# Low-rank token product in one pass, and channel-product blocks of 512, 512, 512, 512 and 256 tokens

## The chip, the cores and the metric

The kernel runs on one core of one Trainium2 chip. The metric is the device time of one execution in microseconds (us), the median of several runs. The engines are TensorE (PE, with its weight loads PEld), VectorE (DVE), ScalarE (ACT), GpSimd (POOL), and SyncE (SP), which here only issues DMAs.

## What is computed

Three layers run one after the other on 4 batches of 576 tokens and 512 channels: rotary attention with 8 heads, a gated layer with a spatial product over tokens, and a mixer. The change touches only the mixer:

```
xt = x.transpose(0, 2, 1)                 # x: 4 x 576 x 512
h = xt @ U @ V                            # U: 576 x 32, V: 32 x 576
u = x + h.transpose(0, 2, 1)
ch = np.maximum(u @ w_ch1, 0.0) @ w_ch2   # w_ch1: 512 x 2048, w_ch2: 2048 x 512
return u + ch
```

All of it is float32. To come near that on TensorE, an operand is split into a high part (rounded to the type float32r) and a low part (what the rounding left), and a product is made of three matmuls: high by high, high by low, low by high.

## The kernel before

Activations lie with channels on the partitions: `X[b]` holds batch b as 128 partitions x 4 channel groups x 576 tokens. The attention layer comes first, with an order written out by hand for all engines. After it the order of TensorE is the order of the code, and a scheduler, which works at build time with a model of the times, sets the order of the other engines and of the DMA queue.

**The gated layer** goes batch by batch, in steps that are named after their tiles in PSUM: `v` (`v_step`, the normed half, 512 columns a matmul), `u` (`u_step`, the gate), `m` (`s_step`, the spatial product), `w` (`o_step`, the output product). The steps of one batch are interleaved with those of the next.

**The low-rank product** of a batch has three steps. `y_step` transposes X (tile `t`) and splits it into YH and YL. `z_step` multiplies both with `U4` and adds them up in one PSUM tile `z`: U4 holds four groups of 32 columns, so the 128 rows of `z` are four products with 32 columns of U each. In the kernel before the groups are U high, U low, U high, U low. Then Z is made: ACT copies the rows of `z` into the rounded type, and DVE replaces rows 64 to 127 by what the rounding left of them. `h_step` (tile `q`) multiplies Z with V. The host stacks V four times, and `VH4` and `VL4` are its high and its low part over all 128 rows; so one `h_step` takes two matmuls over V high and two over V low, of 288 columns each. DVE then adds `q` to X (L680). There are 4 batches with 4 `h_step`s each.

**The channel products** take the 2304 tokens as five blocks that pay no heed to batches: `WIDE` is 472 four times and 416. The 2048 hidden channels form four groups g of 512. For each group and block, `c1` (tile `r`) makes two halves of 24 matmuls each, ACT and DVE turn them into RH and RL (L738, L739), and `c2` (tile `a`) makes two halves of 24 matmuls each, which DVE adds to X (L754). Each matmul has its own weight load. The code runs `c1` of a block between the two halves of `c2` of the block before. Moving operands are UH/UL (the split X of a block; for block 0 they lie in the old tiles XH/XL) and RH/RL (for group 0 and block 0 in the old VH/VL). Weights lie in setA for groups 0 and 2, and in setB for groups 1 and 3; those of the next group are converted on ACT, DVE and POOL while a group runs. In the last group each piece of X is sent out as it is added.

All PSUM tiles after the attention come from one pool of 4 buffers of two banks each, in turn.

The block sizes stand in the code as

```
WIDE = [472] * 4
WIDE.append(NTOK - sum(WIDE))
```

Of the kernel before, what the change touches and what calls it, by code (L numbers as in the profile page):

```python
# [9 lines left out]
F32R = mybir.dt.float32r  # L10
BF16 = mybir.dt.bfloat16
U32 = mybir.dt.uint32
AF = mybir.ActivationFunctionType
ALU = mybir.AluOpType
# [38 lines left out]
def tile_kernel(ctx: ExitStack, tc: tile.TileContext, qk, vv, tabs, w_in, g_ln, wsgT, b_sg, w_out, u_r, v_r, w1, w2, out):  # L53
    nc = tc.nc

    def f(ap):
        return ap.bitcast(F32)

    def h2(ap):
        return ap.rearrange("p (a b) -> p a b", a=2)  # L60
# [20 lines left out]
    B, NHEAD, _, P, S = qk.shape  # L81
# [23 lines left out]
    keep = ctx.enter_context(tc.tile_pool(name="keep", bufs=1))  # L105
# [3 lines left out]
    XH = keep.tile([P, KT, S], F32R, name="XH")  # L109
    XL = keep.tile([P, KT, S], F32R, name="XL")  # L110
    U4 = keep.tile([P, NC, 4, 32], F32R, name="U4")
    VH4 = keep.tile([P, S], F32R, name="VH4")
    VL4 = keep.tile([P, S], F32R, name="VL4")


    es1 = ExitStack()
# [222 lines left out]
    def converted(t0, src, n, use):  # L339

        raw = p1.tile([P, 512, 2], U32, tag="raw64", name="raw64", bufs=1)[:, :n]
        t = p1.tile([P, 512], F32, tag="t64", name="t64", bufs=1)[:, :n]
        later(t0, lambda: nc.sync.dma_start(raw.rearrange("p n w -> p (n w)"), src))
        for j, fn in enumerate(from_f64(t, raw) + use(t)):
            later(t0 + CONVERT + j, fn)
# [9 lines left out]
    def u_chunk(t0):  # L355
        def use(t):
            t = t.rearrange("p (c r) -> p c r", r=32)
            return sum((
                (lambda j=j: nc.scalar.activation(U4[:, :, 2 * j], t, AF.Copy),
                 lambda j=j: nc.gpsimd.tensor_tensor(U4[:, :, 2 * j + 1], t, f(U4[:, :, 2 * j]), ALU.subtract))  # L360
                for j in range(2)), ())
        converted(t0, u_r, NC * 32, use)

    def v_chunk(t0, a):
        hs = slice(a * HALF, (a + 1) * HALF)
        converted(t0, v_r[:, 2 * a * HALF:2 * (a + 1) * HALF], HALF, lambda t: (
            lambda: nc.scalar.activation(VH4[:, hs], t, AF.Copy),
            lambda: nc.gpsimd.tensor_tensor(VL4[:, hs], t, f(VH4[:, hs]), ALU.subtract),
        ))

    LAG, T0 = 3, -20
# [44 lines left out]
    for a in range(2):  # L416
        v_chunk(WTICK[2 * KT + 1 + a], a)
# [72 lines left out]
    def ps_tile(name):  # L490
        return ps2.tile([P, 2, 512], F32, tag="ps", name=name)
# [48 lines left out]
    def mm3(ps, pairs, halves):  # L540
        n = len(pairs)
        for j, (l, r) in enumerate(pairs):
            for a in range(halves):
                rr = r[:, a * HALF:(a + 1) * HALF] if halves == 2 else r
                o = ps[:, a, :HALF] if halves == 2 else ps
                nc.tensor.matmul(o, l, rr, start=(j == 0), stop=(j == n - 1))  # L546
# [115 lines left out]
    def z_step(b, s):  # L662
        if s == 0:
            ZS[b] = ps_tile(f"z{b}")
        pz = ZS[b]
        u4 = U4[:, s].rearrange("p a r -> p (a r)")
        for j, y in enumerate(YS.pop((b, s))):
            nc.tensor.matmul(pz[:, 0, :], u4, y, start=(s == 0 and j == 0), stop=(s == NC - 1))
        if s == NC - 1:
            Z = p2.tile([P, 2, DM], F32R, tag="YL", name=f"Z{b}", bufs=2)[:, 0]  # L670
            nc.scalar.activation(Z, pz[:, 0, :], AF.Copy)
            nc.vector.tensor_tensor(Z[64:128], pz[64:128, 0, :], f(Z[64:128]), ALU.subtract)
            ZS[b] = Z

    def h_step(b, d):
        Z = ZS[b]
        ps = ps_tile(f"q{b}_{d}")
        ds_ = slice(d * P, (d + 1) * P)
        mm3(ps, [(Z[:, ds_], VH4), (Z[:, ds_], VL4)], 2)
        nc.vector.tensor_tensor(h2(X[b][:, d]), ps[:, :, :HALF], h2(X[b][:, d]), ALU.add)  # L680


# [1 line left out]
    FPG = FG // P  # L684
    NG = DH // FG
    NBLK = 5
    WIDE = [472] * 4
    WIDE.append(NTOK - sum(WIDE))
    flat = lambda t, n: t.rearrange("p a b -> p (a b)")[:, :n].rearrange("p (a b) -> p a b", a=KT)
    UH, UL = [flat(XH, KT * WIDE[0])], [flat(XL, KT * WIDE[0])]  # L690
    W = {}
# [11 lines left out]
    def spans(blk):  # L703

        first = t = sum(WIDE[:blk])
        end = t + WIDE[blk]
        while t < end:
# [13 lines left out]
    def c1(g, blk, i):  # L721

        if i == 0:
            RS[g, blk] = (
                (flat(VH, FPG * WIDE[0]), flat(VL, FPG * WIDE[0])) if (g, blk) == (0, 0) else
                [p3.tile([P, FPG, max(WIDE)], F32R, tag=t, name=t, bufs=2)[:, :, :WIDE[blk]] for t in ("RH", "RL")]
            )
# [52 lines left out]
    for b in range(B - 1):  # L780
# [12 lines left out]
        if n < B - 1:  # L793
            run(y_step, b, 0, 2)
            v_step(n, 4)
            us = iter(range(KT))
            if n % 2:
                u_step(n, next(us))
            run(z_step, b, *range(NC - 1))
            y_step(b, 4)  # L800
            u_step(n, next(us))
            z_step(b, 4)
            u_step(n, next(us))
            run(h_step, b, 0, 1)
            u_step(n, next(us))
            run(h_step, b, 2, 3)
            run(u_step, n, *us)
        else:
            v_step(n, 4)
            w = weights(p2, 0, SETA[2:] + SETA[:2])  # L810
            for k0 in range(KT):
                u_step(n, k0)
                next(w)
    a, b = B - 2, B - 1
    for d in range(KT):
# [3 lines left out]
        if d == 1:  # L819
            u_split(0)  # L820
    run(z_step, a, *range(NC - 1))
    y_step(a, 4)
    c1(0, 0, 0)
    for e in range(KT):
        o_step(b, e)
        next(w)
        if e == 0:
            z_step(a, 4)
    run(h_step, a, *range(KT))
    run(y_step, b, 0, 2)  # L830
    c1(0, 0, 1)
# [87 lines left out]
```

## Time and profile before

| | us |
|---|---|
| median of 3 runs | 974.88 |
| the runs | 973.26, 974.88, 978.32 |
| span of the profiled execution, from its first to its last instruction | 971.3 |
| PE busy | 937.9 (97%) |
| DVE busy | 522.0 (54%) |
| POOL busy | 380.1 (39%) |
| ACT busy | 345.3 (36%) |

The profiled execution shows its own time as the span alone. The median of the runs stands 3.6 us above it; that is taken as what lies around the span. The page's groups give a mean duration of one instruction, and for matmuls that is no pace: one of 472 columns lasts 0.37 us on the page, but the next begins 0.21 us after it, since they overlap. A pace is read from a chain of matmuls: its length over their count. In the trace's names a matmul `q<-VH4,Z` writes tile q from the moving operand VH4 with the weights Z.

### The profile page before, as it was taken

How to read it: one execution, taken by the hardware profiler on the slowest of the kernel's cores; microseconds unless marked ns; L12 is line 12 of the kernel's file. 1: busy time of each engine (PE TensorE's matmuls, PEld its weight loads, DVE VectorE, ACT ScalarE, POOL GpSimd, SP SyncE). 2: the span in 40 equal slices, each digit the busy share in tenths (PEclk: the TensorE clock that was granted, in tenths of full speed). 3: DMA queues.
4: the chain of work that ended last, by engine and by line, in shares of the span. 5: the costliest groups of instructions: out<-in, count | busy, mean ns of one | idle time of the engine just before them, and what ended most of it. 6: DMA issues, size and time to landing. Idle time of an engine off the chain costs nothing.

```text
span 971.3 us, 13254 instructions
## 1 busy us (share of the span) xinstructions
PE 937.9 (97%) x5212; PEld 815.4 (84%) x5212; DVE 522.0 (54%) x721; ACT 345.3 (36%) x549; POOL 380.1 (39%) x325
## 2 busy tenths in 40 slices
PE   6899999999999999999999899999999999999998
PEld 3687777777877888999999798899889988998897
DVE  7777877787774387334328846643552542212222
ACT  4366655665657353323215323221321321010010
POOL 7768777887743495231427533210210120000000
PEclk8999999999999999999999999999999999999999
DMA  6577777777750500000003002220220110000112
GB/s 176 146 183 178 189 195 177 191 195 164 187 116 24 161 26 1 1 1 9 15 23 109 22 22 65 87 65 1 87 87 1 66 44 1 1 1 21 60 40 76
DMA packets 58947, 78.00 MB, mean 80 GB/s; under 512 B 31403, under 2 KB 35270, under 8 KB 58886
## 3 DMA queue, kind: packets, MB, share of 16 engines
q1 hardware_dynamic: 58576, 77.08, 29.3%
q8 instruction: 41, 0.67, 0.3%
q14 instruction: 20, 0.16, 0.1%
q10 hardware_dynamic: 310, 0.08, 0.0%
HBM read 55.02 MB, written 4.79 MB: 62 GB/s over the span
## 4 chain that ended last, share of the span: by engine, by line
PE 75%; DVE 13%; DMA 5%; issue 3%; POOL 2%; ACT 1%; SPq 1%; DVEq 0%; POOLq 0%; ACTq 0%
PE a L546 21%; PE r L546 20%; PE pv L274 10%; PE st L246 6%; PE w L546 5%; PE m L546 3%; PE sm L217 3%; PE u L546 3%; PE v L546 3%; DVE MX L222 2%; DMA Q<-K 2%; DVE X L326 1%; DVE t L75 1%; DVE t L74 1%; DVE t L72 1%
## 5 line engine op out<-in xcount | busy, mean ns | idle before, releaser
L222 DVE TENSOR_REDUCE MX<-sm 128x1 f32<-128x576 f32 (+1 forms) x160 | 118.7, 748 | 60.7 <-PE sm L217 58.0
L274 PE MATMUL pv<-pc,VV 128*65 128x288 f32 x512 | 144.7, 405 | 0.5 <-DVE sums L295 0.5
L246 PE MATMUL st<-Q,K 65*128 65x288 f32 (+3 forms) x640 | 126.9, 320 | 7.6 <-DVE MX L222 5.4
L246 PEld LDWEIGHTS st<-Q,K 65*128 65x128 f32 (+3 forms) x640 | 95.7, 179 | 22.3 <-DVE MX L222 8.3
L738 ACT ACTIVATE RH<-r 128x944 fp32r<-128x944 f32 (+1 forms) x38 | 35.7, 939 | 211.4 <-PE r L546 211.4
L739 DVE SCALAR_TENSOR_TENSOR RL<-r,RH 128x944 fp32r<-128x944 f32 (+1 forms) x38 | 42.5, 1117 | 126.2 <-ACT RH L738 126.2
L249 ACT ACTIVATE pc<-st 128x576 f32<-128x576 f32 x128 | 82.6, 646 | 62.8 <-PE st L246 60.6
L546 PE MATMUL a<-RH,setB 128*128 128x472 f32 (+1 forms) x320 | 95.6, 371 | 0.0
L754 DVE TENSOR_TENSOR X<-a,X 128x416 f32<-128x416 f32 (+4 forms) x65 | 46.4, 745 | 91.0 <-PE a L546 90.9
L274 PEld LDWEIGHTS pv<-pc,VV 128*65 128x65 f32 x512 | 68.6, 137 | 29.5 <-DVE sums L295 0.7
L217 PE MATMUL sm<-K,Q 128*128 128x288 f32 (+1 forms) x320 | 77.0, 325 | 13.1 <-ACT Q L193 5.6
L546 PE MATMUL a<-RH,setA 128*128 128x472 f32 (+1 forms) x288 | 86.0, 370 | 0.0
L546 PE MATMUL r<-UH,setB 128*128 128x472 f32 (+1 forms) x256 | 76.4, 369 | 0.0
L546 PE MATMUL r<-UH,setA 128*128 128x472 f32 (+1 forms) x256 | 76.2, 370 | 0.0
L217 PEld LDWEIGHTS sm<-K,Q 128*128 128x128 f32 (+1 forms) x320 | 50.6, 183 | 23.9 <-ACT Q L193 6.8
L546 PEld LDWEIGHTS a<-RH,setB 128*128 128x128 f32 x320 | 60.2, 188 | 6.9
L510 POOL TENSOR_TENSOR setB<-t,setB 128x512 fp32r<-128x512 f32 x16 | 20.6, 1290 | 103.1 <-ACT setB L699 60.4
L546 PE MATMUL a<-RL,setB 128*128 128x472 f32 (+1 forms) x160 | 59.6, 372 | 0.0
L546 PEld LDWEIGHTS a<-RH,setA 128*128 128x128 f32 x288 | 54.1, 188 | 6.1
L150 POOL TENSOR_TENSOR raw<-raw,tab 128x576 f32<-128x576 f32 x31 | 51.9, 1674 | 4.5 <-DMA raw<-in_qk 4.5
L546 PE MATMUL a<-RL,setA 128*128 128x472 f32 (+1 forms) x144 | 53.4, 371 | 0.0
L149 POOL TENSOR_TENSOR raw<-raw,tab 128x576 f32<-128x576 f32 x30 | 47.6, 1587 | 14.8 <-DMA raw<-in_qk 14.8
(172 smaller groups left out, 1968.0 us busy)
## 6 DMA issues: line engine op xcount, KB each, us to landing
raw<-in_qk SPq DMA_DIRECT2D x31, 576.0 KB
Q<-K SPq DMA_DIRECT2D x87, 144.0 KB
raw<-in_w SPq DMA_DIRECT2D x24, 512.0 KB
VV<-in_vv SPq DMA_DIRECT2D x32, 160.0 KB
rb<-rr SPq DMA_DIRECT2D x15, 288.0 KB
K<-K SPq DMA_DIRECT2D x29, 144.0 KB
raw<-in_w_in SPq DMA_DIRECT2D x8, 512.0 KB
gt<-in_w SPq DMA_DIRECT2D x8, 512.0 KB
```

The costliest lines, as they stand in the source:

```text
L149: lambda: e.tensor_tensor(raw[:, 0], raw[:, 0], tab[:, 0], ALU.mult),
L150: lambda: e.tensor_tensor(raw[:, 1], raw[:, 1], tab[:, 1], ALU.mult),
L217: nc.tensor.matmul(ps[:TS[t], n, :HALF], Q1[:, t * P:t * P + TS[t]], K1[:, n * HALF:(n + 1) * HALF], start=True, stop=True)
L222: nc.vector.tensor_reduce(MXs[h % 2][:TS[t], t:t + 1], ps[:TS[t], :, :HALF], AX.XY, ALU.max)
L246: nc.tensor.matmul(ps[:kk, n, :HALF], l[:, c * P:c * P + kk], r[:, ns], start=st, stop=not st)
L249: nc.scalar.activation(h2(pc[:kk]), ps[:kk, :, :HALF], AF.Exp, scale=0.125)
L274: nc.tensor.matmul(o, l, r, start=(c == 0 and j == 0), stop=(c == NC - 1 and j == len(pr) - 1))
L510: return nc.gpsimd.tensor_tensor(out, a, b, ALU.subtract)
L546: nc.tensor.matmul(o, l, rr, start=(j == 0), stop=(j == n - 1))
L738: nc.scalar.activation(RH[:, s], ps[:, :, :WIDE[blk]], AF.Relu)
L739: nc.vector.scalar_tensor_tensor(RL[:, s], ps[:, :, :WIDE[blk]], 0.0, f(RH[:, s]), ALU.max, ALU.subtract)
L754: nc.vector.tensor_tensor(X[b][:, e2, xs], ps[:, :n, us], X[b][:, e2, xs], ALU.add)
```

## The change

U4's groups become U high, U low, U high, U high. VH4 and VL4 become one tile V4: V high in rows 0 to 95, V low (by a subtraction of 32 rows) in rows 96 to 127. DVE now replaces only rows 64 to 95 of Z by what the rounding left. So the four groups of rows give (U high) by V high, (U low) by V high, the remainder of (U high) by V high, and (U high) by V low, in one pass: one `h_step` has two matmuls where it had four. The remainder of the U low rows is no longer multiplied, nor are the products of the low rows with V low.

The blocks of the channel products are 512 four times and 256.

```diff
     U4 = keep.tile([P, NC, 4, 32], F32R, name="U4")
-    VH4 = keep.tile([P, S], F32R, name="VH4")
-    VL4 = keep.tile([P, S], F32R, name="VL4")
+    V4 = keep.tile([P, S], F32R, name="V4")
...
-            return sum((
-                (lambda j=j: nc.scalar.activation(U4[:, :, 2 * j], t, AF.Copy),
-                 lambda j=j: nc.gpsimd.tensor_tensor(U4[:, :, 2 * j + 1], t, f(U4[:, :, 2 * j]), ALU.subtract))
-                for j in range(2)), ())
+            return tuple(lambda j=j: nc.scalar.activation(U4[:, :, j], t, AF.Copy) for j in (0, 2, 3)) + (
+                lambda: nc.gpsimd.tensor_tensor(U4[:, :, 1], t, f(U4[:, :, 0]), ALU.subtract),
+            )
...
-            lambda: nc.scalar.activation(VH4[:, hs], t, AF.Copy),
-            lambda: nc.gpsimd.tensor_tensor(VL4[:, hs], t, f(VH4[:, hs]), ALU.subtract),
+            lambda: nc.scalar.activation(V4[:, hs], t, AF.Copy),
+            lambda: nc.gpsimd.tensor_tensor(V4[96:, hs], t[96:], f(V4[96:, hs]), ALU.subtract),
...
-            nc.vector.tensor_tensor(Z[64:128], pz[64:128, 0, :], f(Z[64:128]), ALU.subtract)
+            nc.vector.tensor_tensor(Z[64:96], pz[64:96, 0, :], f(Z[64:96]), ALU.subtract)
...
-        mm3(ps, [(Z[:, ds_], VH4), (Z[:, ds_], VL4)], 2)
+        mm3(ps, [(Z[:, ds_], V4)], 2)
...
-    WIDE = [472] * 4
+    WIDE = [512] * 4
```

The number of channel-product matmuls stays: 1536 in the four wide blocks and 384 in the last. Their columns stay too: each token is met 384 times.

With the widths the places of tiles in SBUF move. The start of a tile within 256 bytes, as the built programs place them: setA, XH and XL at 128, U4 at 128, TH and YH at 0 (before and after). UH and UL of blocks 1 to 4, RH, RL and setB stand at 192 after; their rows are 2048 bytes apart there (1024 in block 4), so every row keeps that 192. Before, their rows are 1888 or 1664 bytes apart and begin at many offsets.

On PE, the end of batch 2's output product (w3_3), its `q` steps and the transposes after them; Z2 is the weights, V the moving operand. Before:

```order
L546 MATMUL w3_3_5573<-GL_3435,WOH_3432 128x288 x2
L546 MATMUL w3_3_5573<-GH_3434,WOL_3433 128x288 x2
L546 MATMUL q2_0_5609<-VH4_80,Z2_5498 128x288 x2
L546 MATMUL q2_0_5609<-VL4_81,Z2_5498 128x288 x2
L546 MATMUL q2_1_5615<-VH4_80,Z2_5498 128x288 x2
L546 MATMUL q2_1_5615<-VL4_81,Z2_5498 128x288 x2
L546 MATMUL q2_2_5621<-VH4_80,Z2_5498 128x288 x2
L546 MATMUL q2_2_5621<-VL4_81,Z2_5498 128x288 x2
L546 MATMUL q2_3_5627<-VH4_80,Z2_5498 128x288 x2
L546 MATMUL q2_3_5627<-VL4_81,Z2_5498 128x288 x2
L650 MATMUL t3_0_5633<-ident_61,X3_69 128x128 x8
```

The same place on PE after:

```order
L544 MATMUL w3_3_5556<-GL_3434,WOH_3431 128x288 x2
L544 MATMUL w3_3_5556<-GH_3433,WOL_3432 128x288 x2
L544 MATMUL q2_0_5592<-V4_80,Z2_5481 128x288 x2
L544 MATMUL q2_1_5596<-V4_80,Z2_5481 128x288 x2
L544 MATMUL q2_2_5600<-V4_80,Z2_5481 128x288 x2
L544 MATMUL q2_3_5604<-V4_80,Z2_5481 128x288 x2
L648 MATMUL t3_0_5608<-ident_61,X3_69 128x128 x8
```

Half of the `q` matmuls are gone, here and in the three other batches; nothing stands in their place. All else on PE keeps its order, with new widths in `r` and `a`.

On ACT, about the split of block 0 for the channel products (XH from X), with the last gate activation (ug, from u_3) and the conversion of weights (t, setA). Before:

```order
L614 ACTIVATE ug<-u_2_5181 128x576
L71 ACTIVATE t_5208<-gt 128x512
L71 ACTIVATE t_5244<-gt 128x512
L716 ACTIVATE XH<-X_66 128x1888
L614 ACTIVATE ug<-u_3_5217 128x576
L699 ACTIVATE setA_75<-t_5208 128x512
```

The same place on ACT after:

```order
L612 ACTIVATE ug<-u_2_5164 128x576
L71 ACTIVATE t_5191<-gt 128x512
L71 ACTIVATE t_5227<-gt 128x512
L612 ACTIVATE ug<-u_3_5200 128x576
L714 ACTIVATE XH<-X_66 128x2048
L697 ACTIVATE setA_75<-t_5191 128x512
```

The gate activation now stands ahead of the split, and the split is 2048 elements a partition instead of 1888; the POOL subtraction behind it (XL) is longer in the same measure.

## Rows read from the trace of the kernel before

**Rows 1.** Busy time by stretch: length, busy and count per engine, PEclk, DMA share

```profile
core 0: us, PE busy (x) PEld busy (x) DVE busy (x) ACT busy (x) POOL busy (x), PEclk, DMA share, GB/s
377.00:506.00 129.00, 128.26 (x883) 122.63 (x883) 48.83 (x79) 34.02 (x50) 41.17 (x39) 1.00 0.03 9
506.00:555.00 49.00, 44.72 (x312) 42.64 (x311) 40.62 (x51) 23.19 (x35) 28.84 (x18) 1.00 0.21 65
555.00:587.00 32.00, 32.00 (x183) 29.63 (x183) 14.36 (x18) 7.73 (x9) 11.21 (x5) 0.95 0.06 17
587.00:967.00 380.00, 380.00 (x1824) 341.89 (x1822) 142.54 (x199) 67.84 (x88) 36.45 (x26) 1.00 0.14 44
```

**Rows 2.** Waits of PE from 377 to 620: total us, times, longest

```profile
PE w L546 <- DVE VL L739: 2.5, 1, 2.5
PE m L546 <- DVE g L626: 1.1, 1, 1.1
```

**Rows 3.** Chain that ended last, from 377 to 507: start, length, what

```profile
402.08 1.06 PE q L546 x8
406.32 1.06 PE q L546 x8
...
440.45 5.44 PE v L546 x24
...
447.64 2.79 PE v L546 x12
450.42 1.86 PE z L668 x8
...
506.38 1.04 ACT gt L537
```

**Rows 4.** The same chain, from 554 to its end

```profile
554.72 8.17 PE w L546 x48
562.89 2.12 PE q L546 x16
565.00 1.75 PE t L650 x16
...
584.67 2.12 PE q L546 x16
...
602.25 5.13 PE a L546 x24
...
638.20 4.53 PE r L546 x24
...
953.10 14.25 PE a L546 x72
```

**Rows 5.** DVE in order of time, about the q steps of batches 2 and 3

```profile
562.93 0.76 DVE L638 TENSOR_TENSOR X<-w,X 128x576 f32<-128x576 f32 x1 [2.45 <-PE w L546]
563.60 2.74 DVE L680 TENSOR_TENSOR X<-q,X 128x576 f32<-128x576 f32 x4
...
584.71 1.14 DVE L754 TENSOR_TENSOR X<-a,X 128x944 f32<-128x944 f32 x1 [3.50 <-PE a L546]
585.77 2.74 DVE L680 TENSOR_TENSOR X<-q,X 128x576 f32<-128x576 f32 x4
```

**Rows 6.** POOL in order of time, from 523

```profile
523.43 4.51 POOL L510 TENSOR_TENSOR XL<-X,XH 128x1888 fp32r<-128x1888 f32 x1 [4.12 <-ACT XH L716]
```

**Rows 7.** DVE in order of time, from 523 to 539

```profile
523.84 4.65 DVE L75 SCALAR_TENSOR_TENSOR t<-gt,t 128x512 uint32<-128x512 uint32 x1
...
532.99 0.75 DVE L627 TENSOR_TENSOR g<-g,ug 128x576 f32<-128x576 f32 x1
...
536.79 0.68 DVE L75 SCALAR_TENSOR_TENSOR t<-gt,t 128x512 uint32<-128x512 uint32 x1
...
538.72 1.83 DVE L627 TENSOR_TENSOR g<-g,ug 128x576 f32<-128x576 f32 x1
```

**Rows 8.** DVE at the end of the span, in order of time

```profile
967.37 0.59 DVE L754 TENSOR_TENSOR X<-a,X 128x416 f32<-128x416 f32 x1 [1.68 <-PE a L546]
```

## The prediction

> **What bounds the kernel now.** First the stretches [rows 1]. From 587 to the end PE is busy 380.0 of 380 us at full clock, with DVE at 143 us and the rest far below: this is the stage of the channel products, and every nanosecond of a matmul's pace counts there. From 377 to 506 PE is busy 128.3 of 129 us. Between them, from 506 to 555, it is busy 44.7 of 49 us while DVE has 40.6 and POOL 28.8: here the weights of group 0 are converted beside the last spatial product, and PE waits. The two largest waits [rows 2] are 2.5 us before an output-product matmul, for DVE's RL of block 0 (which at that point is the tile VL, L739), and 1.1 us before a spatial matmul. Behind the first wait the granted clock of the next stretch is 0.95 on average [rows 1], and 48 `w` matmuls take 8.17 us [rows 4], 170 ns each, where 288 columns otherwise go at 2.12 / 16 = 132.5 ns.
>
> The reader is then to see how the chain runs: without a break through PE from 377 to 506, where it passes to ACT, DVE and POOL behind the gate's `v` [rows 3], back to PE at 554.7, and on PE to the end [rows 4]. Work taken off PE before 506 should therefore move what follows: the chain's ACT step at 506.38 starts when PE's `v` ends.
>
> **Paces.** They come from the chain, length over count: 472 columns 5.13 / 24 = 213.8 ns, 416 columns 4.53 / 24 = 188.8 ns [rows 4]. For 512 columns the trace has two answers: 5.44 / 24 = 226.7 ns in `v` with the weights XH/XL, but 2.79 / 12 = 232.5 ns in `v` with the weights TH/TL, and 1.86 / 8 = 232.5 ns in `z` [rows 3]. Per column that is 0.453 at 472, 0.454 at 416 and in the two long paces of 512, and 0.443 in the short one. What tells the short pace from the long one in this program: with the short one the moving tile (setA, at 128) and the weights (XH, at 128) begin at the same place within 256 bytes; with the long one they are 128 apart (setA against TH at 0; YH at 0 against U4 at 128). That is a reading of three rows, and no run has tested it.
>
> **The change part by part.**
>
> *The low-rank product.* 32 matmuls of 288 columns go: 8 a batch, 8 x 132.5 = 1.06 us. In batches 0 and 1 `q` stands in two pairs with gate steps between (each pair now 1.06 us [rows 3], of which half goes), on an unbroken PE chain: 2 x 1.06 = 2.1 us, which I let pass through the stretch 506 to 555, since its chain starts from PE. In batches 2 and 3 the four `q` steps stand together, and the pool of 4 PSUM buffers decides. Batch 2: PE starts `q` at 562.89; the fourth `q` takes the buffer of the last `w`, which DVE frees at 562.93 + 0.76 = 563.7, and the first transpose behind takes that of the first `q`, which DVE frees some 0.7 us later, at 564.3 (2.74 us for four adds [rows 5]). Now the transposes start at 565.0, when PE is through; then at 564.35. Of 1.06 us 0.65 is left. Batch 3: the fourth `q` takes the buffer of the `a` before, whose add on DVE (1.14 us, 1.2 at 512) ends 1.25 us after PE's start; `c1` of block 1 then needs the first `q`'s add behind it: 1.25 + 0.65 = 1.9 us after PE's start, against 2.12 now. 0.2 us is left. Sum: 2.1 + 0.65 + 0.2 = 3.0 us saved, of 4.2 us of matmuls. Bounds: 0.9 (the first 2.1 lost again in the stretch 506 to 555) and 4.2.
>
> *The channel products.* Before: 1536 x 213.8 = 328.3 us and 384 x 188.8 = 72.5 us, together 400.8 us. After there are 1536 of 512 columns and 384 of 256. No row has a matmul of 256 columns; the nearest are 128 columns (the transposes, 1.75 / 16 = 109.4 ns [rows 4]) and 288 columns (132.5 ns). I take half of the 512-column pace, 113.3 or 116.3 ns, since both lie between; the ends would move the sum by about -2 and +7 us. By the reading of the offsets, after the change weights and moving rows agree within 256 bytes in groups 1 and 3 (setB, UH, RH all at 192) but for `c1` of block 0 (XH at 128), and in groups 0 and 2 (setA at 128) only for `c1` of block 0. That is 2 x (144 + 192) + 2 x 48 = 768 of the 1536 wide matmuls, and 192 of the 384 narrow ones. So: 768 x 226.7 + 768 x 232.5 + 192 x 113.3 + 192 x 116.3 = 174.1 + 178.6 + 21.8 + 22.3 = 396.8 us: 4.0 us saved. All at the short pace would be 391.7 (9.1 saved), all at the long one 401.8 (1.0 lost). PE waits for nothing in this stage (380.0 of 380 us busy [rows 1]), and evictions grow by 512/472, about 0.1 us each, behind halves of 5.1 us; block 4's halves shrink to 2.8 us, with DVE and ACT work shrinking in step. I cost that at nothing; the cover is two halves of `c2` or `c1` between a tile's last matmul and its next reader, over 5 us.
>
> *The stretch 506 to 555.* Block 0's split grows: XL on POOL from 4.51 us by 2048/1888 to 4.9 us [rows 6], a price of 0.4 us if the chain stays behind it. While it runs, DVE's L75 lasts 4.65 us [rows 7] where the same form takes 0.68 elsewhere, and it ends 0.55 us after XL does. ACT now does the last gate activation ahead of the split, so XL starts later, about when that L75 does; which of the two is first can change. I take +0.4 us, with bounds of -4 (that L75 is no longer held) and +4 (another instruction is held as well).
>
> The Trainium skill bears this reading out (page "SBUF — State Buffer", section "SBUF: two separate sides"): GpSimd and a DVE instruction with two SBUF inputs share one pair of ports, whoever comes first holds it for a whole instruction, and the other blocks. The rows agree.
>
> *The rest.* U4's third copy goes from POOL to ACT, and V's low part has 32 rows: both lie in the attention stage off PE, at nothing (their own length, under a microsecond, if they were not). The last add shrinks from 0.59 us [rows 8] to some 0.36: -0.2 us.
>
> **Sum.** -3.0 - 4.0 + 0.4 - 0.2 = -6.8 us. The profiled span of 971.3 becomes 964.5; with the same 3.6 us around it, the median of 974.9 becomes **968.1**.
>
> **Rivals.**
>
> *All 512-column matmuls take the short pace.* 226.7 ns would be what full, regular rows of 2048 bytes give, and 232.5 ns pieces that had not settled (they hold 12 and 8 matmuls, the `v` with XH holds 24). Against: nothing in those rows settles within their length. Products -9.1: 968.1 - 5.1 = 963.0.
>
> *Time goes by columns.* 416, 472 and the long pace of 512 all cost 0.453 to 0.454 ns a column, and count and columns of the products stay. Then the products give 0, or +1 by the 232.5 itself: 972.1 to 973.1; only the 3.0 us of `q` are left. For it speaks that three widths agree; against it the `v` row.
>
> The Trainium skill has a rule of this kind (page "TensorE: Matmul & The Clock Gate", section "Back-to-back issue gap"): a warm matmul follows the one before after its columns over 2.4 GHz plus 2.5 ns. By it, too, the products would not change, since a sum of columns and a count do not; its paces, 199 ns at 472 columns and 176 at 416, are 14 and 13 ns below the rows', so the rows decide.
>
> *DVE is held longer.* In the stretch 506 to 555 the DVE chain sets PE's 2.5 us wait. A held L75 costs 4.65 - 0.68 = 4.0 us, a held L627 1.83 - 0.75 = 1.1 us [rows 7]. The scheduler's order of ACT and DVE there has moved, with the longer XL among it. If two more instructions were held as that L75 is, 8 us would come on: 976.1, slower than before, and 977.9 if the clock falls once more as behind the 2.5 us wait (8.17 us against 48 x 132.5 = 6.4 us, 1.8 us). It decides from 6.8 us of further holding on. For it: POOL's instructions are as many and one is longer. Against: the same conversions in nearly the same order, and XL is one instruction, which holds DVE once.
>
> That the matmuls do not go is excluded: the order of PE lacks them.
>
> **How the numbers follow.** Forecast 968.1: 0.43. All short, 963.0: 0.20. By columns, 972 to 973: 0.27. Held, 976 to 978: 0.10. The forecast's own range, from the bounds of the stretch and of 256 columns taken at half their width, is 964.5 to 972. For 8 in 10 the range takes in the first two rivals as far as their middle: **962.0 to 974.0**. About 0.5%, 4.9 us, is what a measurement can tell: faster means below 970.0, slower above 979.8. Faster: most of the forecast (0.34), all of the first rival (0.20) and little of the second: 0.55. Slower needs the held case with products at the long pace: 0.07. Within 0.5%: 0.38.
>
> **What would show it.** `q` as 8 matmuls a batch, with the transposes of batch 3 some 0.65 us earlier relative to the start of `q` and `c1` of block 1 only 0.2 us earlier relative to it. Halves of 24 wide matmuls at 5.44 us in groups 1 and 3 and 5.58 in groups 0 and 2; if both kinds are alike, the reading of the offsets is wrong. Halves of the last block at 2.7 to 2.8 us; 3.2 would mean that 256 columns cost as much as 288. PE without waits from 587 on. A wait of PE near 552 that is much longer than 2.5 us, or a DVE instruction held in other places than behind XL, would make the time miss the forecast upward.

## The result and the profile after

| | before | after |
|---|---|---|
| median of 6 runs each on one chip, us | 973.57 (972.8 to 978.32) | 965.74 (963.3 to 968.37) |
| ratio of after to before, 95% interval | | 0.991 [0.990, 0.993] |
| span of the profiled execution, us | 971.3 | 966.6 |
| PE, DVE, POOL, ACT busy in it, us | 937.9, 522.0, 380.1, 345.3 | 929.6, 524.3, 382.6, 345.8 |

The change makes the kernel 7.8 us faster; 968.1 was forecast, with a range of 962.0 to 974.0.

The profiled spans differ by only 4.7 us. The one of after is the longest of its six executions (966.6; the five others 961.5 to 964.1), and the reason lies ahead of the gated layer, where the change touches only the conversion of U and V: the gated layer's first `v` starts at 321.03 us, against 317.93 before. In further traces, of kernels that differ from after only behind this point, it starts between 316.7 and 321.5. So traces are compared here from this `v` on.

The windows of after, cut where the same steps start and end as in [rows 1] (length, busy time and count of each engine, granted clock, DMA share):

```profile
380.10:506.75 126.65, 126.13 (x866) 120.57 (x866) 48.23 (x78) 34.03 (x50) 40.95 (x38) 1.00 0.03 9
506.75:555.80 49.05, 44.66 (x310) 42.12 (x308) 40.61 (x51) 23.40 (x35) 29.56 (x18) 1.00 0.20 65
555.80:588.60 32.80, 31.96 (x165) 27.45 (x165) 14.34 (x18) 7.88 (x9) 10.93 (x5) 0.95 0.05 16
588.60:963.00 374.40, 374.32 (x1824) 315.78 (x1824) 143.39 (x200) 67.78 (x88) 36.73 (x26) 1.00 0.14 45
```

The picture is that of before: PE is full but for the second stretch, and the clock is again 0.95 behind it. The last row answers to the stretch from 587 to 967: from the first start of its 1824 matmuls to the last it is 374.04 us, where before took 380.35. What PE waited for from 377 to 966 (total, times, longest), beside [rows 2]:

```profile
PE w L544 <- DVE VL L737: 2.5, 1, 2.5
PE w L544 <- POOL GL L508: 2.1, 2, 1.3
PE r L544 <- DVE g L624: 0.9, 1, 0.9
PE t L648 <- DVE X L636: 0.5, 1, 0.5
PE q L544 <- DVE X L752: 0.5, 1, 0.5
...
```

The 2.5 us wait is there unchanged. The wait of `m` for `g` has gone, and one of the first `c1` half (`r`) for `g` has come. The 0.5 us of `t` is not new: before has it at the same place, behind the first batch's output product (at 388.34, in after at 391.10).

```profile
PE t L650 <- DVE X L638: 0.5, 1, 0.5
```

The wait of `q` is new: the `q` steps of batch 3 no longer fill the time that DVE needs to free PSUM buffers. In batch 2 the lost time shows in the chain. The 2.1 us for GL are 1.3 us at 379.85 and 0.8 us at 549.11; the changed kernel again has only the second of them. From the chain of after (start, length, what), beside [rows 3, 4]:

```profile
404.82 0.53 PE q L544 x4
...
408.53 0.53 PE q L544 x4
...
554.53 1.24 DVE VL L737
555.77 0.04 issue
555.81 8.17 PE w L544 x48
564.01 0.76 DVE X L636
564.76 0.67 DVE X L678
565.44 0.04 issue
565.48 1.97 PE t L648 x16
...
581.04 5.61 PE a L544 x24
586.67 1.23 DVE X L752
587.89 0.68 DVE X L678
588.57 0.04 issue
588.61 11.51 PE r L544 x49
599.89 5.49 PE r L544 x24
...
643.83 2.83 PE r L544 x24
...
737.24 5.44 PE a L544 x24
742.68 2.87 PE r L544 x24
...
841.94 2.72 PE r L544 x24
```

In batches 0 and 1 a pair of `q` steps takes 0.53 us instead of 1.06. In batches 2 and 3 the chain now leaves PE around `q` and runs over DVE's adds, as the prediction has it. The halves of the products are told apart by group: 5.49 us / 24 = 228.9 ns in groups 0 and 2 (the rows at 599.89), 5.44 us = 226.7 ns in groups 1 and 3 (at 737.24), and 2.72 to 2.87 us in the last block. On DVE, in order of time, beside [rows 5, 7, 8]:

```profile
524.52 0.69 DVE L75 SCALAR_TENSOR_TENSOR t<-gt,t 128x512 uint32<-128x512 uint32 x1
...
525.98 4.32 DVE L625 TENSOR_TENSOR g<-g,ug 128x576 f32<-128x576 f32 x1
...
962.97 0.42 DVE L752 TENSOR_TENSOR X<-a,X 128x256 f32<-128x256 f32 x1 [1.01 <-PE a L544]
```

and on POOL, beside [rows 6]:

```profile
524.78 4.89 POOL L508 TENSOR_TENSOR XL<-X,XH 128x2048 fp32r<-128x2048 f32 x1 [4.83 <-ACT XH L714]
```

While XL runs, another instruction is held: the product of the gate (L625, L627 before) for 4.32 us, and no longer L75.

Where the time went, from the first `v` on, in the profiled executions (the changed kernel a second time in the last column):

| | before | after | again |
|---|---|---|---|
| first `v` to the last batch's `m` | 200.97 | 198.51 | 198.52 |
| that `m` to `c1` of block 1 | 67.73 | 69.07 | 68.52 |
| of it block 0's four halves | 20.78 | 22.39 | 22.37 |
| `c1` of block 1 to the last matmul's start | 380.35 | 374.04 | 374.04 |
| from there to the end | 4.31 | 3.92 | 3.9 |
| sum | 653.4 | 645.5 | 645.0 |

All pieces go from start to start. The first one takes 197.7 to 198.5 us in the traces of kernels that differ from after only behind it, so tenths of a microsecond in it tell nothing.

### The profile page after: what moved, and what is told of

The parts are those of the page before. It is cut to its first block, busy times and chain, and to the rows that moved or that the text cites. A ratio compares the mean times of both kernels' runs of the same rounds, so it can differ in the third digit from the quotient of the medians.

```text
span 966.6 us, 13198 instructions
## 1 busy us (share of the span) xinstructions
PE 929.6 (96%) x5180; PEld 784.4 (81%) x5180; DVE 524.3 (54%) x721; ACT 345.8 (36%) x550; POOL 382.6 (40%) x324
## 4 chain that ended last, share of the span: by engine, by line
PE 73%; DVE 12%; DMA 8%; issue 3%; POOL 2%; ACT 1%; SPq 1%; ACTq 0%; DVEq 0%; POOLq 0%
PE a L544 20%; PE r L544 20%; PE pv L273 9%; PE st L245 6%; PE w L544 5%; DMA Q<-K 4%; PE m L544 3%; PE u L544 3%; PE v L544 3%; PE sm L216 3%; DVE MX L221 2%; DMA raw<-in_qk 2%; DVE X L325 1%; DVE t L74 1%; DVE g L625 1%
## 5 line engine op out<-in xcount | busy, mean ns | idle before, releaser
L736 ACT ACTIVATE RH<-r 128x1024 fp32r<-128x1024 f32 (+1 forms) x38 | 35.5, 935 | 207.2 <-PE r L544 207.2
L737 DVE SCALAR_TENSOR_TENSOR RL<-r,RH 128x1024 fp32r<-128x1024 f32 (+1 forms) x38 | 42.3, 1112 | 123.8 <-ACT RH L736 123.7
L752 DVE TENSOR_TENSOR X<-a,X 128x256 f32<-128x256 f32 (+4 forms) x65 | 46.4, 744 | 90.8 <-PE a L544 90.7
L544 PE MATMUL a<-RH,setB 128*128 128x512 f32 (+1 forms) x320 | 93.3, 368 | 0.0
L544 PE MATMUL a<-RH,setA 128*128 128x512 f32 (+1 forms) x288 | 83.8, 367 | 0.0
L544 PE MATMUL r<-UH,setA 128*128 128x512 f32 (+1 forms) x256 | 73.1, 364 | 0.1
L544 PE MATMUL r<-UH,setB 128*128 128x512 f32 (+1 forms) x256 | 73.2, 363 | 0.0
L544 PEld LDWEIGHTS a<-RH,setB 128*128 128x128 f32 x320 | 58.2, 188 | 10.0
L544 PE MATMUL a<-RL,setB 128*128 128x512 f32 (+1 forms) x160 | 58.9, 368 | 0.0
L149 POOL TENSOR_TENSOR raw<-raw,tab 128x576 f32<-128x576 f32 x31 | 51.6, 1664 | 5.1 <-DMA raw<-in_qk 5.1
L544 PEld LDWEIGHTS r<-UH,setA 128*128 128x128 f32 x256 | 46.1, 188 | 8.2 <-DVE X L678 0.4
```

The costliest lines, as they stand in the source:

```text
L149: lambda: e.tensor_tensor(raw[:, 1], raw[:, 1], tab[:, 1], ALU.mult),
L736: nc.scalar.activation(RH[:, s], ps[:, :, :WIDE[blk]], AF.Relu)
L737: nc.vector.scalar_tensor_tensor(RL[:, s], ps[:, :, :WIDE[blk]], 0.0, f(RH[:, s]), ALU.max, ALU.subtract)
L752: nc.vector.tensor_tensor(X[b][:, e2, xs], ps[:, :n, us], X[b][:, e2, xs], ALU.add)
```

## Experiments

In each, the times are medians of runs that share a chip with runs of the kernel before (973.37 us beside the first four below, 972.98 beside the next four, 972.03 beside the last two). The diffs are against the changed kernel.

**One part alone: the low-rank product.**

```diff
-    WIDE = [512] * 4
+    WIDE = [472] * 4
```

> The one-pass low-rank product alone; blocks stay 472 and 416. Working theory (q saves 2.1 us in batches 0 and 1, 0.4 to 0.65 in batch 2, 0 to 0.2 in batch 3; the blocks save 4.7 us of the rest): 2.5 to 3 us below the kernel before, ratio 0.997. Halves of 24 matmuls at 472 columns stay near 5.13 us. In batch 3 the first matmul of c1 of block 1 starts about 2.0 us after the start of q, as before, though q has half the matmuls. Rival (all 32 matmuls count in full, the blocks give 3.6 us): 4.2 us below. Rival (the low-rank part gives nothing, since the stretch 506 to 555 takes it back): within 1 us of before.

969.82 us, 0.996 [0.994, 0.997]: 3.6 us below before, a little more than expected. In the trace the piece up to the last `m` is 198.53 us (2.44 shorter), the next one 66.97 (0.76 shorter), and the products take 401.4 us where before took 401.3. The low-rank product alone is worth some 3.2 us there.

**The other part alone.** The `q` matmuls are back in number, over V4 twice, so that the low-rank term counts double.

```diff
-        mm3(ps, [(Z[:, ds_], V4)], 2)
+        mm3(ps, [(Z[:, ds_], V4), (Z[:, ds_], V4)], 2)
```

> The changed kernel with each q product issued twice over the same V4 (so the low-rank term is added twice and the output differs): the 32 matmuls are back, the blocks stay 512 and 256. Working theory: 2.5 to 3 us above the changed kernel, so some 5 to 5.5 us below the kernel before. Rival (q in full): 4.2 us above the changed kernel, 4 us below the kernel before.

967.67 us, 0.996 [0.994, 0.997]. That is 1.9 us above the changed kernel, less than the 2.5 to 3 expected. The piece up to the last `m` is 200.61 us, 2.1 longer than in the changed kernel; the products take 396.3 us (396.6 in after). So 2.1 us of matmuls in batches 0 and 1 do pass through to the end, and the two parts add up to within a microsecond: from the first `v` on they save 3.2 and 5.7 us alone, and 7.8 to 8.4 together. In batch 3 the chain of this kernel stays on PE:

```profile
588.96 2.12 PE q L544 x16
```

From the first `q` to `c1` of block 1 it is 2.14 us with these 16 matmuls, and 2.14 us with the 8 of after: there the removed matmuls gave nothing.

**The reading of the offsets.** An unused tile ahead of UH shifts UH, UL, RH, RL and setB alone. With 48 elements all of them come to 128 within 256 bytes, where setA, XH and XL stand; with 16 they come to 0, which leaves groups 1 and 3 in agreement and puts groups 0 and 2 128 bytes apart.

```diff
     p3u = ctx.enter_context(tc.tile_pool(name="p3u", bufs=1, reuse_waits="tile"))
+    p3u.tile([P, 48], F32, name="pad")
```

> The changed kernel with 192 unused bytes ahead of UH1: UH, UL, RH, RL and setB then begin at 128 within 256 bytes, as setA, XH and XL do. Theory of the offsets: every half of 24 matmuls of 512 columns takes 5.44 us (226.7 ns a matmul) but for c2 of group 0, block 0 (weights setA, moving VH at 0); groups 0 and 2, now 228.9 ns, fall to 226.7, and c1 of block 0 in groups 1 and 3 from 233.3 to 226.7: 2 us below the changed kernel. Rival (the pace belongs to the tiles, setA low in memory and setB high, whatever the offsets): paces as in the changed kernel, 228.9 with setA and 226.7 with setB, and the same time.

965.38 us, 0.992 [0.990, 0.994]. From the chain of this kernel, in group 0:

```profile
614.58 5.44 PE a L544 x24
620.02 5.44 PE r L544 x24
...
641.78 2.87 PE r L544 x24
```

The halves of group 0 fall from 5.49 to 5.44 us and those with setB and XH from 233.3 to 226.7 ns a matmul, as the reading of the offsets wants it. But the last block goes to 2.87 us (119.7 ns) everywhere. The products are 395.3 us, 1.3 less than in after, where 2 were expected; the medians (965.38 and 965.74) don't tell the two kernels apart.

```diff
+    p3u.tile([P, 16], F32, name="pad")
```

> The changed kernel with 64 unused bytes ahead of UH1: UH, UL, RH, RL and setB begin at 0 within 256 bytes, 128 apart from setA, XH and XL. Theory of the offsets: groups 1 and 3 stay at 226.7 ns (all at 0), groups 0 and 2 rise from 228.9 to about 232.5 (128 apart, as v with TH and z): 2 to 2.5 us above the changed kernel. Rival (tiles, not offsets): paces and time as in the changed kernel.

968.57 us, 0.996 [0.994, 0.998]. The chain of this kernel, in group 0 and, at 738.62, in group 1:

```profile
617.07 5.57 PE a L544 x24
622.64 5.58 PE r L544 x24
...
738.62 5.44 PE a L544 x24
```

Halves with setA and UH or RH are at 5.57 to 5.60 us (232.1 to 233.3 ns), those with setB stay at 5.44. The products are 399.2 us, 2.6 more than in after, where 2 to 2.5 were expected, and 3.9 more than with 48 elements. Nothing but the place of tiles differs between the two, so at 512 columns the place decides between 226.7 ns and 232 to 233; what was taken from three rows of before is shown for these two places.

**Is it the place, or the regular rows?** The tiles of the 48-element kernel, with only 472 of each 512 columns computed (40 columns of every wide block are left out).

```diff
-            mm3(ps[:, a, :WIDE[blk]], pr, 1)
+            w = min(WIDE[blk], 472)
+            mm3(ps[:, a, :w], [(l, r[:, :w]) for l, r in pr], 1)
...
```

> The kernel with the same offset everywhere, where the matmuls of the four wide blocks, their evictions and their adds take only the first 472 of the 512 columns of each row (40 tokens of each block are left out, so the output is not the reference's). It tells apart what gives the 226.7 ns: rows that all begin at the same place within 256 bytes, or the full width of 512. Theory of the rows: 472 x 226.7 / 512 = 209.0 ns a matmul, a half of 24 in 5.02 us. Rival (a regular pace needs the full 512 columns): 213.5 to 214 ns as in the kernel before, 5.13 us a half. The 256-column matmuls stay near 119.7 ns.

939.51 us in a single run, with the work left out; its trace is read for the pace alone. From its chain:

```profile
616.72 5.12 PE a L544 x24
```

5.12 / 24 = 213.3 ns, or 0.452 ns a column: what 472 columns took before (213.8) on irregular rows, and not the 0.443 of 512 columns. The agreement of places gives nothing at 472 columns; of these two widths only 512 has the short pace.

**Spreading the `q` steps.** Those of batches 2 and 3 go in pairs between the output product's last steps and between the quarters of `c2`.

```diff
+        if e > 1:
+            run(h_step, a, 2 * e - 4, 2 * e - 3)
-    run(h_step, a, *range(KT))
...
-    c2(0, 0, 1)
-    run(h_step, b, *range(KT))
+    c2(0, 0, 2, 1)
+    run(h_step, b, 0, 1)
+    c2(0, 0, 3, 1)
+    run(h_step, b, 2, 3)
```

> The changed kernel with the q steps of batch 2 as two pairs, one ahead of the last output-product step and one behind it, and those of batch 3 as two pairs with the last quarter of c2 of block 0 between: as much work, but DVE frees a PSUM buffer while PE has other work. Theory of the PSUM buffers: from the start of q to c1 in batch 3, now 2.14 us for 8 matmuls, 1.06 us are left, and in batch 2 another 0.4 to 0.7 us go: 1.3 to 1.7 us below the changed kernel. Rival (PE waits there for something else, such as Z): no change.

963.92 us, 0.991 [0.989, 0.993]. From its chain:

```profile
581.23 2.78 PE a L544 x12
584.01 0.53 PE q L544 x4
584.54 16.80 PE r L544 x72
...
606.95 5.60 PE r L544 x24
...
772.57 5.49 PE r L544 x24
```

All `q` together now take 4.24 us, 32 x 132.5 ns, instead of 5.94, and the piece from the last `m` to `c1` of block 1 falls from 68.52 to 67.26. So what `q` lost in batches 2 and 3 was the wait for PSUM buffers. But the halves of group 0 run at 5.60 us here (the row at 606.95), with the same addresses that give 5.49 in after and, at 772.57, in group 2 of this kernel too; from `c1` of block 1 on the products are 0.8 us longer. So at 64 bytes apart the place alone does not fix the pace, and of the 1.3 to 1.7 us expected the median shows 0.6 (964.55 for the changed kernel beside it).

**The longest holder.** Block 0's XL on POOL in four instructions instead of one.

```diff
-            less(UL[blk][:, :, us], x, f(hi))
+            for k in range(KT) if blk == 0 else [slice(0, KT)]:
+                less(UL[blk][:, k, us], x[:, k], f(hi[:, k]))
```

> The changed kernel with the subtraction XL of block 0 as four POOL instructions of 512 elements instead of one of 2048. Theory (one long POOL instruction holds one DVE instruction to its end, and the DVE chain sets PE's wait near 553): the product with the gate, which now lasts 4.32 us beside XL, falls below 2 us, and the stretch from the last gate's v to the w matmuls behind the wait (49.1 us) shortens by 1 to 3 us. Rival (four short instructions hold DVE as long in sum as one long one, or another engine sets the wait): the stretch stays within 0.5 us.

960.51 us, 0.988 [0.986, 0.990]; the changed kernel beside it gave 964.55. On POOL and on DVE:

```profile
521.17 6.37 POOL L508 TENSOR_TENSOR XL<-X,XH 128x512 fp32r<-128x512 f32 x4 [4.78 <-ACT XH L714]
```

```profile
522.37 1.01 DVE L625 TENSOR_TENSOR g<-g,ug 128x576 f32<-128x576 f32 x1
```

XL as a whole takes longer, 6.37 us instead of 4.89, and yet L625 lasts 1.01 us instead of 4.32: it is let in between two pieces. PE's waits, its windows (the first ends 2.9 us into the `w` behind the wait) and the chain from there on:

```profile
PE w L544 <- POOL GL L508: 1.8, 2, 1.3
PE w L544 <- DVE VL L738: 1.7, 1, 1.7
```

```profile
503.20:552.40 49.20, 47.01 (x332) 45.08 (x331) 38.05 (x53) 25.24 (x36) 31.65 (x22) 1.00 0.20 65
552.40:580.70 28.30, 27.50 (x145) 23.00 (x144) 12.25 (x15) 6.29 (x7) 9.65 (x4) 1.00 0.06 19
```

```profile
549.47 6.66 PE w L544 x48
```

The wait of `r` for `g` is gone, the wait for VL is 1.7 us instead of 2.5, and behind it the clock stays at 1.00: 48 `w` take 6.66 us, where they take 7.98 in the changed kernel beside it and 8.17 in after. From the end of the last gate's `v` (503.20) to these `w` it is 46.3 us instead of 49.1, within the expected 1 to 3 us. From the last `m` to `c1` of block 1 it is 64.75 us, 3.8 less than in the changed kernel beside it: 1.1 at the wait of `r`, 2.2 in the last 72 `w` (0.8 of wait, the rest clock), 0.3 in the `w` before, 0.2 in `z`. The rule of the Trainium skill that the prediction names (page "SBUF — State Buffer", section "SBUF: two separate sides": the pair of ports is held for a whole instruction) agrees with both sides of this, 4.32 us beside one long instruction and 1.01 beside four short ones.

**The changed kernel again**, without any edit, beside the two runs above.

> The changed kernel as it is, beside the other runs: some 8 us below the kernel before. Its trace tells whether the attention stage, which began the gated layer 3.1 us later in the first trace of the changed kernel than in the one before, does so again. Theory (it differs from execution to execution): the first v within 317.5 to 321.5 us of the start, in no relation to the kernel. Rival (the change delays it): 321 us again.

964.55 us, 0.992 [0.990, 0.994]. The waits of PE for VL (2.5 us) and of `r` for `g` (0.9), the clock of 0.95 behind, and all paces are those of after. The first `v` starts at 316.72, 4.3 us earlier: a little outside the expected range, but the rival, that the change delays it, falls.

**All together.** XL in pieces, `q` in pairs, and the 48-element tile.

> The changed kernel with three edits at once: block 0's XL subtraction on POOL in four pieces, the q steps of batches 2 and 3 in pairs with other matmuls between them, and an unused tile of 192 bytes a partition ahead of UH, which puts all weights and moving rows of groups 1 to 4 at the same place within 256 bytes. Theory that the three are independent: the XL pieces alone gave 960.5; pairs take 1.3 us more off the path from m of batch 3 to the first half of c1; the products fall from 396.6 us to about 395.5 (wide matmuls all at 226.7 to 228 ns, the last block at 119.7). Sum 958.0, between 957 and 959.5. Rival, that the pieces and the pairs free the same wait: 959.5 to 960.5, with no further gain between m and c1 over the pieces alone.

959.65 us (955.42 to 960.04), 0.987 [0.984, 0.989], just above the expected 957 to 959.5 and inside the range of the rival. The trace tells the two apart. From the first `v` to the last matmul the trace has 633.8 us, against 636.5 with the pieces alone: 1.6 less between `m` and `c1`, where the rival wanted no gain, and 1.4 less in the products (395.1 us). So the three are independent, within a few tenths, in the trace. The median shows only 0.9 of these 2.7 us; that is within the spread of when the first `v` starts, which the runs don't separate.

Then the same with block 4 alone placed 64 bytes from the weights (this diff is against the kernel with all three edits; padB brings setB, RH and RL back to their place within 256 bytes):

```diff
-                [p3.tile([P, FPG, max(WIDE)], F32R, tag=t, name=t, bufs=2)[:, :, :WIDE[blk]] for t in ("RH", "RL")]
+                [at(p3.tile([P, FPG, max(WIDE)], F32R, tag=t, name=t, bufs=2), 16 * (blk == NBLK - 1), WIDE[blk]) for t in ("RH", "RL")]
...
     for i in range(1, NBLK):
+        if i == NBLK - 1:
+            p3u.tile([P, 16], F32, name="pad4")
...
+    p3.tile([P, 48], F32, name="padB")
+    at = lambda t, o, w: t.rearrange("p a b -> p (a b)")[:, o:o + FPG * w].rearrange("p (a b) -> p a b", a=FPG)
```

> The kernel of e10, and block 4 alone (256 columns) with its moving rows 64 bytes on from the weights within 256 bytes. Theory that at 256 columns the same place is the dearer one (119.7 ns) and 64 bytes apart the cheaper one (113.3 to 117.8): 384 matmuls gain 2 to 6 ns each, 0.8 to 2.4 us, so 956.4 us, between 955.5 and 957.5, and halves of the last block of 2.72 to 2.83 us in place of 2.87. Rival, that 119.7 came from what runs before a half and not from the place: no difference from e10, halves at 2.87 us.

958.1 us (957.1 to 960.03), 0.986 [0.984, 0.988], a little above the forecast of 955.5 to 957.5. In its chain:

```profile
630.59 5.44 PE a L544 x24
636.03 2.83 PE r L544 x24
```

The last block's halves are 2.83 us (117.9 ns) instead of 2.87, in all groups, and the products 394.5 us. So at 256 columns the same place is dearer than 64 bytes apart, and the rival falls; the cheap 113.3 ns that `c1` of group 2 has in after (2.72 us) did not come. The times of the last two kernels can't be told apart. This one has the lowest median of all, 14 us below before; by the profiles it is 17 from the first `v` to the end (636.5 against 653.4). The built program puts setB, RH and RL 256 bytes from UH and UL within 512 here, and the wide halves stay at 5.44 us: agreement within 256 bytes is enough.

## Why the prediction was right, and where its terms were off

| step | forecast, us | measured in after (again) |
|---|---|---|
| `q`, batches 0 and 1 | -2.1 | -2.1 |
| `q`, batch 2 | -0.65 | -0.4 (-0.4) |
| `q`, batch 3 | -0.2 | 0.0 (0.0) |
| products | -4.0 | -4.7 (-4.7) |
| stretch 506 to 555 | +0.4 | +0.1 (-0.4) |
| tail | -0.2 | -0.4 (-0.4) |
| in no term: the rest up to the last `m` | 0 | -0.3 (-0.3) |
| sum | -6.8 | -7.8 (-8.4) |

Here the stretch is what is left of the piece from `m` to `c1` of block 1 without block 0's halves and without `q`; the sums are of the unrounded pieces. The -0.3 in no term is within the spread of the first piece between executions.

**The low-rank product** was sized well where PE's chain is unbroken. The step that failed is the one for batches 2 and 3. The mechanism was right (PE is through and waits for DVE's adds to free a buffer: the `q` steps in pairs lose nothing, and in batch 3 16 `q` matmuls take no longer than 8), but the moment from which the waits were reckoned was 0.16 us late: the prediction took PE's start of `q` from the chain, 562.89 and 584.67, where the chain puts the modelled end of the matmul before. The records of `q` start at 562.73 and 584.51. Reckoned from there, the add of 1.23 us and the 0.68 us behind it in batch 3 end just when PE had been through before, and nothing is left; in batch 2 0.4 us is left.

**The channel products** came out 0.7 us better than forecast. Two kinds of halves in the groups forecast for them are what the reading of the offsets wanted, and the kernels with 48 and 16 elements settle it for the same place against 128 bytes apart. The size was off in two terms that partly cancel, so the sum is closer than its terms by luck. In groups 0 and 2 most wide matmuls take 228.9 ns, not 232.5: the prediction knew two places, agreement and 128 apart, and gave the pace of 128 apart to tiles that are 64 apart. And 256 columns cost 118.2 ns on average instead of 114.8; with the same place, where half of the short pace was taken, they cost 119.7, more than with 64 apart. On average a wide matmul took 228.6 ns instead of the forecast's 229.6, which is -1.5 us over 1536; the narrow ones are +1.3 us over 384; and before's products are 401.3 us by the records, where the rounded paces gave 400.8.

| most halves of 24 matmuls, moving rows against weights within 256 bytes | 512 columns, ns | 256 columns, ns |
|---|---|---|
| same place | 226.7 | 119.7 |
| 64 apart | 228.9 (UH, RH with setA) or 233.3 (XH with setB; UH, RH with setA in group 0 of the kernel with pairs) | 113.3 or 117.6 to 117.9 |
| 128 apart | 232.1 to 233.8 | 118.3 to 119.9 |

The rival that all wide matmuls are at the short pace falls by the groups 0 and 2 of after (228.9), the rival that time goes by columns by 226.7 in groups 1 and 3; at 472 columns the latter holds even with agreeing places (213.3).

**The stretch 506 to 555.** XL takes 4.89 us, as forecast. That L75 might no longer be held and another instruction might be were the two bounds of that term; both happened at once, and the 4.3 us of L625 stand in place of the 4.65 of L75. That the two bounds cancel was luck; the +0.4 did not forecast it. `g` (L624) behind it is again late, and as it frees a PSUM buffer, one PE step waits for it: 1.1 us `m` before, 0.9 us `r` now, and `r` starts 20.1 us behind the last `m` before, 20.4 and 20.1 now. The price of the longer XL doesn't show: the change measures +0.1 and -0.4 us in two executions, and with XL at its old length (the low-rank product alone) it is -0.3. The rival of several held instructions had its mechanism right and its count wrong: XL is one instruction and holds one. The four pieces show what that one costs, 3.8 us, of which some 1.3 is clock.

**The time around the span.** The prediction took 3.6 us, the distance from the profiled span to the median of before's three runs, for what lies around the span. That is 1.8: of after's profiled execution both are given, 968.37 and 966.6. By the same 1.8 the profiled execution of before took 973.1, which is 1.8 below that median. The reading was wrong, but the sum does not suffer by it, since the same 3.6 us lead from the median to the span and back: the forecast is the median of three runs less 6.8. Of the miss of 2.4 us, 1.3 is that median (974.88; six runs give 973.57) and 1.0 the sum, 6.8 against the 7.8 measured.

## What to carry to other kernels

Count a removed matmul as a gain only as far as the evictions behind it free their PSUM buffers in time, from the first record's start and not from the chain's; where they don't, put other matmuls between instead of standing all steps in a row. A long GpSimd instruction on the way of a VectorE chain is worth cutting into pieces, even if the pieces together take longer. And when widths change, look where weights and moving rows begin within 256 bytes: at 512 columns the same place was worth 2 to 3% of a pace against 128 apart and 1% against 64 apart, at no cost but an unused tile. Over all products that was 1.3 us of 396.6, too little for the median to show.

## What was not expected of the hardware

- The pace of 512 columns depends on where weights and moving rows begin: 226.7 ns on the same place, 232.1 to 233.8 ns 128 bytes apart; at 256 columns the same place (119.7 ns) is no better than 128 apart, and 64 apart is cheaper (113.3 to 117.9 ns). Why is open.
- 64 bytes apart, the same addresses gave 228.9 ns in after and 233.3 ns in group 0 of the kernel with `q` in pairs, while group 2 of that kernel was at 228.9 (5.49 us a half). The last block's `c1` in group 0 took 117.8 ns in after and 113.3 in the kernel with the `q` matmuls back, again at the same addresses. What ran before has a hand in it; what in it, no run tells.
- The granted clock was 0.95 on average (1.2 GHz for a part, 2.4 for the rest) in the stretch behind PE's wait of 2.5 us in before, after and the changed kernel again. It fell there in all eight traces with a wait of 2.4 to 2.6 us, and stayed at 1.00 in the three kernels with XL in pieces, behind waits of 1.6 to 1.7 us at the same place.
- The attention ended up to 4.8 us earlier or later in executions of kernels that don't differ up to that point. Its cause was not looked for.
